# The order of eleven matmuls in the first gates of a gated unit, beside a long convolution on one core

## The chip, the core and the metric

The kernel runs on one core of one Trainium2 chip. The metric is the device time of one execution in microseconds (us). TensorE (PE) multiplies; its weight loads are listed apart (PEld). VectorE (DVE), ScalarE (ACT) and GpSimd (POOL) compute on tiles, SyncE (SP) starts transfers. The engines run side by side and wait for one another.

## The reference

The input x (2048 tokens of 448 numbers) is normalised per token. Two branches read the normalised tokens xn, and the output is the sum of x and both:

```python
xn = _layernorm(x, axis=-1)
return x + _A_ref(xn, ...) + _B_ref(xn, B_w_gate, B_w_up, B_w_down)
# A: a long convolution over the tokens, its kernel K made of 256 complex
#    exponentials per channel, done with FFTs of length 4096, plus u * D_skip
# B: the gated unit
g = jnp.einsum("bsd,df->bsf", x, w_gate)
u = jnp.einsum("bsd,df->bsf", x, w_up)
h = _sigmoid(g) * u
return jnp.einsum("bsf,fd->bsd", h, w_down)
```

The gated unit has 448 inputs, 1792 hidden units and 448 outputs.

## The kernel before, in words

**Two streams of work.** The convolution (`conv`) and the gated unit (`glu`) are two Python generators. A loop at the end of `s4d_glu_kernel` takes a step from the one that has done the smaller share of its work, so that the code's order interleaves them. That order is not the final one: the program is built with `schedule_with_timeline_sim=True`, so a planner lays out each engine's list of instructions. It takes planned durations and picks, whenever an engine is free in the plan, the ready instruction of the highest priority. Priority follows the order of the code; `hp()` moves an instruction 300 places ahead, and `tc.issue_after(i)` keeps an instruction behind another one on its engine. Once laid out, each engine's list is fixed, and the engine works it off in order.

**Stages.** First the tokens are loaded, normalised, transposed and split (0 to some 40 us). Meanwhile `prep` computes the exponents of the convolution kernel on DVE, ACT and POOL, up to about 124 us. Then `kgen` makes the kernel K chunk by chunk (TensorE at L524 and L600, DVE at L586 to L588), to about 540 us. Then `spectra` multiplies in the frequency domain and transforms back (L883, L910, L945). The gated unit fills TensorE throughout.

**The gated unit.** It takes 1024 tokens at a time (`half` 0 and 1), as two blocks t = 0 and 1 of 512 tokens, and runs over 14 slices f of 128 hidden units, in groups of three or two (`FCH`). For each (f, t) `gate` computes the two products of a slice, gate (i = 0) and up (i = 1), each in one PSUM bank `gu` (four buffers). Then ACT computes `th` (a tanh, L701), DVE `hf` (L704), ACT `hh` (L709) and DVE `hl` (L711). After a group, L801 multiplies with w_down into `po`, and DVE adds it to `acc` (L806). In half 0 the first group's order is (f 0, t 0), (f 1, t 0), (f 0, t 1), (f 1, t 1), and so on; t = 1 comes with the second block of tokens.

**Split numbers.** Each float32 operand is kept as a high part in a reduced format and a low remainder, and a product is the sum of high x high, high x low and low x high. The 448 inputs are three rows of 128 (index k) and one of 64. For the three: `xh[:, k]` and `xl[:, k]`. For the 64 that are left, `xr` holds the high part in partitions 0 to 63 and the low part in 64 to 127, so one matmul does both. Weights are `wh` and `wl`; `wh` is made by ACT from the loaded weights (L743), `wl` by DVE (L745 or L747).

**How x comes.** `x_transpose` transposes four blocks of 128 tokens with TensorE (L210). For each k, ACT copies the high part (L219) and DVE subtracts for the low part (L220); last come xr's high half by ACT (L222) and its low half by DVE (L223). For the first tokens (t = 0) and the second (t = 1) this is done at the start of the kernel.

**The order in a gate.** Each of the two accumulations is eleven matmuls in one bank, in the order of a list: wh x xh (k = 0, 1, 2), wh x xr, wl x xh (three), wl x xr, wh x xl (three).

Of the kernel before, what the change touches and what calls it, by code (L numbers as in the profile page):

```python
# [130 lines left out]
def s4d_glu_kernel(ctx, tc, io):  # L131
# [488 lines left out]
    def w_load(f, raw=None, eng=nc.sync):  # L620
        fs = slice(128 * f, 128 * f + 128)
        if raw is None:
            raw = pg.tile([128, 2, 4, 128], F32, name="wraw", bufs=1)
        for i, nm in enumerate(("B_w_gate", "B_w_up")):
            w = io[nm]
            eng.dma_start(raw[:, i, 0:3], w[0:384, fs].rearrange("(k p) f -> p k f", p=128))
            for h in range(2):
                eng.dma_start(raw[64 * h : 64 * h + 64, i, 3], w[384:448, fs])
        return raw

    def rd_load(f, rd=None, eng=nc.sync):
        if rd is None:
            rd = pg.tile([128, D], F32, name="rd", bufs=RB)
        eng.dma_start(rd, io["B_w_down"][128 * f : 128 * f + 128])
        return rd

    def w_low():
        return pg.tile([128, 2, 4, 128], F32R, name="wl", bufs=2)

    def d_low():  # L640
        return pg.tile([128, D], F32R, name="dl", bufs=FCH[0] + 1)

    def kept(t, d, f):
        for i in range(2):
            flat = t[i].rearrange("p i k f -> p (i k f)") if len(t[i].shape) == 4 else t[i]
            yield flat.bitcast(F32), d[i, f]
# [29 lines left out]
            for i in range(2):  # L676
                nc.scalar.dma_start(x1_d[:, row(b + i, g)], to[64 * i : 64 * i + 64])

    def gate(w, xs, to, between=None, behind=False):
        wh, wl = w  # L680
        xh, xl, xr = xs
        pgu = []
        for i in range(2):
            ps = psg.tile([128, 512], F32, name="gu", bufs=4)
            mm = [(wh[:, i, k], xh[:, k]) for k in range(3)]
            mm += [(wh[:, i, 3], xr)]
            mm += [(wl[:, i, k], xh[:, k]) for k in range(3)]
            mm += [(wl[:, i, 3], xr)]
            mm += [(wh[:, i, k], xl[:, k]) for k in range(3)]
            order = turns if behind and i == 1 else sp_mm if glu_on else None  # L690
            with tc.issue_after(order[0].ins) if order else nullcontext():
                for n, (a_, b_) in enumerate(mm):
                    glu_mm[:] = [nc.tensor.matmul(ps, a_, b_, start=(n == 0), stop=(n == len(mm) - 1))]  # L693
            pgu.append(ps)
            if i == 0:
                yield 2.5
                if between:
                    between()
        th = pg.tile([128, 512], F32, name="th", bufs=1)
        with hp(HP):  # L700
            marks[0] = nc.scalar.activation(th, pgu[0], AF.Tanh, scale=0.5)  # L701
        hf = pg.tile([128, 512], F32, name="hf", bufs=1)
        with hp(HP):
            marks[1] = v.scalar_tensor_tensor(hf, th, 1.0, pgu[1], ALU.add, ALU.mult)  # L704
        hfs.append(marks[1])
        hh = pg.tile([128, 512], F32R, name="hh", bufs=2 * FCH[0])
        hl = pg.tile([128, 512], F32R, name="hl", bufs=2 * FCH[0])
        with hp(HP):
            nc.scalar.copy(hh, hf)  # L709
        with hp(HP):  # L710
            v.tensor_tensor(hl, hf, hh, ALU.subtract)  # L711
        to.append((hh, hl))

    def glu():
        for half in range(2):
# [4 lines left out]
            for fs_ in ORDER[half]:  # L720
                fc, f0 = len(fs_), fs_[0]
                wts, ws, hs = [], [], [[], []]
# [12 lines left out]
                for n_, (f, t) in enumerate(order):  # L735
                    if t == 0:
                        wh = pg.tile([128, 2, 4, 128], F32R, name="wh", bufs=2)
                        if half == 0:
                            first = len(raws) == 2
                            raw, rd = raws.pop() if raws else (w_load(f), None)  # L740
                            wl = w_low()
                            with hp(HP):
                                nc.scalar.copy(wh, raw)  # L743
                                if first:
                                    v.scalar_tensor_tensor(wl, raw, lim[:, 0, 0:1], wh, ALU.mult, ALU.subtract)  # L745
                                else:
                                    v.tensor_tensor(wl, raw, wh, ALU.subtract)  # L747
                            if f not in RAW:
                                for t_, d_ in kept((wh, wl), wt_d, f):
                                    nc.sync.dma_start(d_, t_)  # L750
                        elif f in RAW:
                            raw, wl = w_load(f, eng=nc.gpsimd), w_low()
                            nc.gpsimd.tensor_copy(wh, raw)
                            nc.gpsimd.tensor_tensor(wl, raw, wh, ALU.subtract)
                        else:
                            wl = w_low()
                            for t_, d_ in kept((wh, wl), wt_d, f):
                                nc.sync.dma_start(t_, d_)
                        ws.append((wh, wl))
                    between = (lambda s_=mid[n_]: step(*s_)) if cross and mid[n_] else None  # L760

                    yield from gate(ws[f - f0], xq[2 * half + t], hs[t], between, half == 0 and (f, t) == (1, 0))
                    if t == 0:
                        dh = pg.tile([128, D], F32R, name="dh", bufs=FCH[0])
                        if half == 0:
                            rd = rd or rd_load(f)
                            dl = d_low()
                            with hp(HP), tc.issue_after((act if f == 1 else marks)[0].ins):
                                nc.scalar.copy(dh, rd)
                            nc.gpsimd.tensor_tensor(dl, rd, dh, ALU.subtract)  # L770
                            if f not in RAW:
                                for t_, d_ in kept((dh, dl), dt_d, f):
                                    nc.sync.dma_start(d_, t_)
                        elif f in RAW:
                            dl = d_low()
                            rd = rd_load(f, pg.tile([128, D], F32, name="rdw", tag="wraw", bufs=1), nc.gpsimd)
                            nc.gpsimd.tensor_copy(dh, rd)
                            nc.gpsimd.tensor_tensor(dl, rd, dh, ALU.subtract)
                        else:
                            dl = d_low()  # L780
                            for t_, d_ in kept((dh, dl), dt_d, f):
                                nc.sync.dma_start(t_, d_)
                        wts.append((dh, dl))
                    yield 2.5
                    for s_ in end[n_] if cross else ():
                        step(*s_)
                    if cross:
                        yield 2
# [304 lines left out]
    xq, psc, raws, acl, marks, slots, pqs = list(x_first), [], [], [], [None, None], {}, []  # L1093
    W1s, GGs, act = [], [], []
    gens = [conv(), glu()]
    total = [sum(Y0) + 11 * WP + 8 * WX + 34 + NCK * WK + HOLE + 17 * WS, 2 * (4 + NFT * 14.8) - HELD]
    done = [0.0, 0.0]
    done[0] += next(gens[0])
    held = False
    while any(g is not None for g in gens):  # L1100
# [4 lines left out]
        try:  # L1105
            w = next(gens[i])
# [31 lines left out]
```

## Time and profile before

| What | Value |
|---|---|
| Median of three runs | 751.43 us (747.39 to 751.76) |
| The profiled execution, its own time | 754.2 us |
| Its span, first to last instruction | 752.3 us |
| Mean granted TensorE clock | 0.983 |
| ACT busy | 421.6 us (56%) |
| HBM read, written | 69.64 MB, 43.84 MB |
| Mean transfer rate | 153 GB/s |

A row of the timeline gives the start in us, the length in us, the engine, the line of the code, the operation, the written tile and the read tiles with their shapes, a count if several were merged, and in brackets the idle time before it with what ended it. Merged rows of matmuls show the length of the group. The lengths of matmuls overlap, as they are pipelined: the distance of their starts says what one costs. A row of the waits names the waiting line, what it waited for, the total, the number of times and the longest. Waits are inferred from semaphore events; where several were awaited, the last counts.

### The profile page before, as it was taken

The page shows a single profiled execution, that of the slowest core. Times are in us where ns is not written, and L with a number is a line of the kernel's source. Part 1 is how long each engine was busy: PE and PEld are TensorE (multiplying, and loading weights), DVE is VectorE, ACT ScalarE, POOL GpSimd, SP SyncE. Part 2 cuts the span into 40 slices and gives each one's busy share as a digit, 9 for nine tenths or more (in the row PEclk, how much of TensorE's full clock was granted, in tenths as well). Part 3 has the DMA queues.
Part 4 walks back from the last instruction along what each step waited for, and adds up shares of the span by engine and source line. Part 5 has one row for each costly group of instructions (what it writes and reads, how often), then busy time and mean ns, then how long its engine had stood idle before and what let it go on. Part 6 is the DMA issues. An engine that isn't in the chain of part 4 may idle for free.

```text
span 752.3 us, 19390 instructions
## 1 busy us (share of the span) xinstructions
PE 703.2 (93%) x7892; PEld 552.4 (73%) x7892; DVE 559.1 (74%) x776; ACT 421.6 (56%) x650; POOL 343.9 (46%) x423
## 2 busy tenths in 40 slices
PE   3898998999999999999999999999899999997994
PEld 2665787887777886666878887888777787775783
DVE  5899995689789989758668888878964554663553
ACT  3546383587687878785576776777543222322310
POOL 2110074865786885747346676566445002520001
PEclk9998999999999999999999999999999999999998
DMA  9956357254144442466722223122158999999756
GB/s 206 232 143 172 96 152 225 70 170 144 49 135 138 146 120 94 144 160 186 240 95 90 81 98 117 52 90 87 30 153 245 253 248 230 247 246 237 160 152 168
DMA packets 90760, 114.75 MB, mean 153 GB/s; under 512 B 11888, under 2 KB 78640, under 8 KB 90416
## 3 DMA queue, kind: packets, MB, share of 16 engines
q1 hardware_dynamic: 79056, 89.11, 43.9%
q10 hardware_dynamic: 9040, 18.24, 8.2%
q0 software_dynamic: 2576, 6.17, 3.1%
q8 instruction: 62, 1.02, 0.6%
q14 instruction: 26, 0.21, 0.1%
HBM read 69.64 MB, written 43.84 MB: 151 GB/s over the span
## 4 chain that ended last, share of the span: by engine, by line
PE 63%; DVE 14%; DMA 9%; ACT 4%; issue 4%; SPq 3%; POOL 2%; ACTq 0%; DVEq 0%; POOLq 0%
PE gu L693 25%; PE po L801 13%; PE ko L600 7%; PE tr L524 6%; PE sp L883 5%; PE pv L910 3%; DMA v_d<-vt 2%; DVE Et L587 2%; DVE Et L586 2%; DMA vp<-v_d 2%; DVE Ft L588 2%; DVE pm L438 1%; PE kp L551 1%; DMA sx<-x_d 1%; DMA skl<-sk_d 1%
## 5 line engine op out<-in xcount | busy, mean ns | idle before, releaser
L501 POOL TENSOR_TENSOR me<-me,pm 128x32 f32<-128x32 f32 (+1 forms) x168 | 136.5, 813 | 128.1 <-DVE Et L587 116.3
L501 POOL TENSOR_TENSOR mf<-mf,pm 128x64 f32<-128x64 f32 (+1 forms) x112 | 105.5, 942 | 4.5
L693 PE MATMUL gu<-xh,wh 128*128 128x512 f32 x336 | 99.1, 402 | 2.3 <-DVE acc L806 1.1
L693 PE MATMUL gu<-xl,wh 128*128 128x512 f32 x336 | 97.0, 392 | 0.0
L693 PE MATMUL gu<-xh,wl 128*128 128x512 f32 x336 | 96.4, 393 | 0.0
L586 DVE TENSOR_TENSOR Et<-me,S 128x1024 f32<-128x1024 f32 x56 | 81.3, 1451 | 18.9 <-ACT S L536 15.5
L587 DVE TENSOR_TENSOR Et<-me,S 128x1024 f32<-128x1024 f32 x56 | 80.6, 1439 | 19.6 <-ACT me L514 18.2
L801 PE MATMUL po<-dh,hh 128*128 128x448 f32 x224 | 85.9, 383 | 2.1 <-DVE hf L704 2.1
L533 ACT ACTIVATE S<-tr 128x1024 f32<-128x1024 f32 x56 | 57.7, 1031 | 49.0 <-PE tr L524 42.6
L801 PE MATMUL po<-dl,hh 128*128 128x448 f32 x224 | 83.8, 374 | 0.0
L801 PE MATMUL po<-dh,hl 128*128 128x448 f32 x224 | 83.0, 372 | 0.0
L588 DVE TENSOR_TENSOR Ft<-mf,S 128x1024 f32<-128x1024 f32 x56 | 76.4, 1364 | 6.1 <-PE ko L600 4.4
L709 ACT CAST hh<-hf 128x512 fp32r<-128x512 f32 x56 | 35.0, 624 | 80.2 <-DVE hf L704 70.0
L600 PEld LDWEIGHTS ko<-Et,Ft 128*32 128x32 f32 x3584 | 54.2, 110 | 31.8 <-issue 17.1
L693 PEld LDWEIGHTS gu<-xh,wh 128*128 128x128 f32 x336 | 61.4, 189 | 20.9 <-issue 5.1
L600 PE MATMUL ko<-Et,Ft 128*32 128x64 f32 x3584 | 65.7, 221 | 10.7 <-DVE Ft L588 6.2
L693 PEld LDWEIGHTS gu<-xh,wl 128*128 128x128 f32 x336 | 63.4, 189 | 14.4 <-DVE pl L309 0.7
L693 PEld LDWEIGHTS gu<-xl,wh 128*128 128x128 f32 x336 | 63.0, 188 | 14.2 <-issue 0.7
L524 PE MATMUL tr<-sel,ph 128*128 128x512 f32 x224 | 66.0, 416 | 3.5 <-DMA ph<-ph_d 2.2
L536 ACT ACTIVATE S<-S,hpi 128x1024 f32<-128x1024 f32 x56 | 65.4, 1168 | 0.0
L806 DVE SCALAR_TENSOR_TENSOR acc<-po,acc 128x448 f32<-128x448 f32 x80 | 48.0, 615 | 23.4 <-PE po L801 23.2
L704 DVE SCALAR_TENSOR_TENSOR hf<-th,gu 128x512 f32<-128x512 f32 x56 | 38.2, 681 | 34.9 <-PE gu L693 33.7
(198 smaller groups left out, 1299.3 us busy)
## 6 DMA issues: line engine op xcount, KB each, us to landing
sk_d<-sk ACTq DMA_DIRECT2D x14, 512.0 KB
sx<-x_d SPq DMA_DIRECT2D x32, 224.0 KB
skl<-sk_d SPq DMA_DIRECT2D x16, 448.0 KB
vp<-v_d SPq DMA_DIRECT2D x16, 448.0 KB
v_d<-vt SPq DMA_DIRECT2D x62, 112.0 KB
wt_d<-wh SPq DMA_DIRECT2D x9, 512.0 KB
wt_d<-wl SPq DMA_DIRECT2D x9, 512.0 KB
wl<-wt_d SPq DMA_DIRECT2D x9, 512.0 KB
```

Source lines behind the costliest of these rows:

```text
L501: ins = nc.gpsimd.tensor_tensor(m[:, :, w + a : 2 * w : n], m[:, :, a:w:n], par(base + i).unsqueeze(2).to_broadcast([128, 4 * DC, w // n]) ...
L524: nc.tensor.matmul(ps[:, h], ph[:, cn % 2, 128 * h : 128 * h + 128], sel[:, i], start=(i == 0), stop=(i == 1),)
L533: nc.scalar.activation(rows(cs), pv, AF.Abs)
L536: sins[:] = [nc.scalar.activation(cs, cs, AF.Sin, scale=-TWO_PI, bias=hpi)]
L586: v.tensor_tensor(Et[:, :, :, 32:64], two(me[:, :, 32:64]), S[:, 1::-1], ALU.mult)
L587: v.tensor_tensor(Et[:, :, :, 0:32], two(me[:, :, 0:32]), S[:, 1:3, :, ::-1], ALU.mult)
L588: fts[:] = [v.tensor_tensor(Ft, two(mf), S[:, 3:5], ALU.mult)]
L600: mm = nc.tensor.matmul(ko[32 * j : 32 * j + 32, sl], Ft[:, cc, DC * h + 4 * q + j], Et[:, cc, DC * h + 4 * q + j], start=(k == 0), stop=( ...
L693: glu_mm[:] = [nc.tensor.matmul(ps, a_, b_, start=(n == 0), stop=(n == len(mm) - 1))]
L704: marks[1] = v.scalar_tensor_tensor(hf, th, 1.0, pgu[1], ALU.add, ALU.mult)
L801: glu_mm[:] = [nc.tensor.matmul(po, a_[:, bs], w_, start=(n == 0), stop=(n == 3 * fc - 1))]
L806: v.scalar_tensor_tensor(acc[:, b], po, 0.5, acc[:, b], ALU.mult, ALU.add)
```

## The change

`gate` gets an argument `first`. The call in `glu` sets it for slice f = 0 in half 0, so for two calls: (f 0, t 0) and (f 0, t 1). In these, each of the two accumulations (i = 0 and 1) takes its eleven matmuls in another order: wh x xh (three), wl x xh (three), wh x xl (three), wh x xr, wl x xr. The same eleven products are summed, in another order. The first of the list starts the accumulation and the last closes it, as before. All other gates keep their order.

```diff
-    def gate(w, xs, to, between=None, behind=False):
+    def gate(w, xs, to, between=None, behind=False, first=False):
...
             mm += [(wh[:, i, k], xl[:, k]) for k in range(3)]
+            if first:
+
+                mm = mm[:3] + mm[4:7] + mm[8:] + mm[3:8:4]
             order = turns if behind and i == 1 else sp_mm if glu_on else None
...
-                    yield from gate(ws[f - f0], xq[2 * half + t], hs[t], between, half == 0 and (f, t) == (1, 0))
+                    yield from gate(ws[f - f0], xq[2 * half + t], hs[t], between, half == 0 and (f, t) == (1, 0), half == 0 and f == 0)
```

## The prediction

> **What bounds the kernel now.** I read the page first, then the table of windows by stage, TensorE's waits in the first 41 us, the timeline there, and last the chain of work. The page's span and engine shares:
>
> ```profile
> span 752.3 us, 19390 instructions
> PE 703.2 (93%) x7892; PEld 552.4 (73%) x7892; DVE 559.1 (74%) x776; ACT 421.6 (56%) x650; POOL 343.9 (46%) x423
> ```
>
> The table of windows (window, length, then busy time of each engine, granted clock, DMA share, GB/s):
>
> ```profile
> 16.30:30.00 13.70, 12.84 (x60) 9.96 (x60) 10.53 (x29) 10.58 (x19) 2.13 (x6) 1.00 1.07 237
> 30.00:41.00 11.00, 7.96 (x33) 6.04 (x33) 10.94 (x21) 4.43 (x8) 1.15 (x1) 1.00 0.86 200
> 41.00:60.00 19.00, 18.10 (x94) 12.04 (x93) 19.00 (x40) 8.15 (x12) 1.83 (x1) 1.00 0.57 161
> 60.00:83.00 23.00, 20.17 (x98) 14.81 (x98) 23.00 (x44) 16.61 (x26) 0.20 (x1) 0.85 0.51 136
> 150.00:545.00 395.00, 383.97 (x5472) 305.09 (x5471) 326.35 (x346) 288.46 (x423) 250.22 (x298) 0.99 0.37 118
> 640.00:690.00 50.00, 45.55 (x420) 33.28 (x417) 29.78 (x54) 12.87 (x26) 16.15 (x18) 0.97 1.01 243
> 690.00:753.00 63.00, 52.54 (x458) 41.13 (x457) 27.96 (x55) 12.10 (x23) 4.38 (x8) 0.96 0.69 165
> ```
>
> TensorE is busy for 703.2 of 752.3 us, so 49 us of idleness is all that a change of order can touch. It is full in the long middle (384 of 395 us), and idle at the start and in the tail. From 30 to 83 us DVE is the engine without a gap (10.94 of 11, then 19.00 of 19 and 23.00 of 23): it works through the normalisation, the gates' epilogues and the preparation of the convolution. TensorE waits for it there. The change touches only the two gates of the unit's first group f = 0 in half 0, at 16 to 25 us and at 30 to 41 us. What TensorE waits for between 16 and 41 us (waiting line, releaser, total, times, longest):
>
> ```profile
> PE gu L693 <- DVE xr L223: 2.7, 1, 2.7
> PE gu L693 <- ACT xh L219: 0.7, 1, 0.7
> PE gu L693 <- ACT wh L743: 0.4, 1, 0.4
> ```
>
> **The change part by part.** No instruction is added or removed; 11 matmuls in each of four accumulations change places. No DMA is moved, nothing on SP's or POOL's queue is passed, and no matmul gets a new input. So the price of the matmuls themselves is nothing, and all that counts is which wait each meets. The two that read xr move from places 4 and 8 to 10 and 11. What is queued behind them on TensorE now runs ahead of the wait for xr.
>
> First tile. The timeline's rows (start, length, engine, line):
>
> ```profile
> 12.90 1.28 DVE L745 SCALAR_TENSOR_TENSOR wl<-wraw,lim,wh 128x1024 fp32r<-128x1024 f32 x1
> 16.33 1.94 PE L693 MATMUL gu<-xh,wh 128*128 128x512 f32 x6
> 17.17 0.86 PE L693 MATMUL gu<-xh,wh 128*128 128x512 f32 x3
> 18.08 0.68 DVE L220 TENSOR_TENSOR xl<-kp,xh 128x512 fp32r<-128x512 f32 x1
> 18.71 0.97 PE L693 MATMUL gu<-xh,wh 128*128 128x512 f32 x3 [0.45 <-ACT wh L743]
> 18.86 0.69 DVE L223 TENSOR_TENSOR xr<-gu,xr 64x512 fp32r<-64x512 f32 x1
> 19.60 0.50 PE L693 MATMUL gu<-xr,wh 128*128 128x512 f32 x1
> 19.94 0.86 PE L693 MATMUL gu<-xh,wl 128*128 128x512 f32 x3
> 22.83 1.90 DVE L268 TENSOR_SCALAR xn<-acc,ys,zs 128x448 f32<-128x448 f32 x2
> 24.49 0.85 PE L693 MATMUL gu<-xl,wh 128*128 128x512 f32 x3
> 25.18 0.27 PE L210 MATMUL tr<-ident,xn 128*128 128x128 f32 x1
> 26.82 0.27 PE L210 MATMUL gu<-ident,xn 128*64 128x128 f32 x1
> 28.16 0.57 ACT L701 ACTIVATE th<-gu 128x512 f32<-128x512 f32 x1
> 29.71 0.69 DVE L704 SCALAR_TENSOR_TENSOR hf<-th,gu 128x512 f32<-128x512 f32 x1 [1.78 <-PE gu L693]
> ```
>
> Six matmuls run (three for each of the gate's two banks; the third starts at 17.17), then three of the next group as soon as its wh is there at 18.71, then the first xr at 19.60, right after DVE's xr ends at 19.55. So 9 are issued before 19.60, 24 after it. Twenty start between 19.94 and 24.49, so one costs 4.55/20 = 0.2275 us. In the new order a bank needs wl (there since 14.18) and then xl (the last ends at 18.76) before xr. From 17.17 on nothing holds TensorE: by 19.60 it would have issued 2 + 2.43/0.2275 = 12.7 instead of 9, which is 3.7 x 0.2275 = 0.84 us, and the restart after the xr wait (0.34 from 19.60 to 19.94 instead of 0.2275) adds 0.11. I take 0.95 us. Is it hidden? The sixteen transposes behind (25.18 to 26.82) wait only for xn, whose last piece DVE ends at 24.73; the other three pieces are earlier. Started 0.95 earlier, twelve transposes last until about 25.4, so xn does not hold the other four. Then come 11 gate matmuls, and hf at 29.71, for which DVE had idled 1.78 us. Its other input th ends at 28.73, so hf comes at 28.76: the whole 0.95 passes to DVE, which is full from there to 83 us. This term lies on the path.
>
> Second tile:
>
> ```profile
> 30.30 2.34 PE L693 MATMUL gu<-xh,wh 128*128 128x512 f32 x9 [0.69 <-ACT xh L219]
> 33.92 0.69 DVE L220 TENSOR_TENSOR xl<-kp,xh 128x512 fp32r<-128x512 f32 x1
> 34.64 0.68 DVE L223 TENSOR_TENSOR xr<-gu,xr 64x512 fp32r<-64x512 f32 x1
> 35.38 0.50 PE L693 MATMUL gu<-xr,wh 128*128 128x512 f32 x1 [2.74 <-DVE xr L223]
> ```
>
> Nine matmuls, then 2.74 us of waiting for xr. In the new order six with wl and most of the six with xl fill it: 12 x 0.2275 = 2.7 us of work comes forward. That is cover, not gain, if DVE sets the pace behind it. TensorE's waits from 41 to 83 us, from 83 to 125 us, and two rows of DVE's groups from 30 to 83 us:
>
> ```profile
> PE po L801 <- DVE hf L704: 2.1, 1, 2.1
> PE tr L279 <- ACT x1ab L290: 1.0, 1, 1.0
> ...
> PE tr L524 <- DMA ph<-ph_d: 2.2, 1, 2.2
> PE gu L693 <- DVE acc L806: 1.1, 1, 1.1
> ...
> L747 DVE TENSOR_TENSOR wl<-wraw,wh 128x1024 fp32r<-128x1024 f32 x3 | 3.6, 1195 | 0.0
> L704 DVE SCALAR_TENSOR_TENSOR hf<-th,gu 128x512 f32<-128x512 f32 x5 | 3.4, 674 | 1.8 <-PE gu L693 1.8
> ```
>
> In its old order TensorE already waits for DVE's hf (2.1) and acc (1.1) before 84 us. A TensorE that is 2.7 us ahead waits 2.7 us longer at the same places. I price the second tile at 0 and keep -2.7 as the end of the range, for the case that its lead is kept.
>
> The part with no row is the order of everything else. Each engine's list is laid out from planned durations and priorities: the six-then-three sequence above, against the code's sequence of eleven, shows that the plan moves matmuls past one another. An earlier gate in the plan moves later instructions on all engines. I bound this by the tail's transfers (rival 3), and take 0, the value nearest to the full middle, where TensorE has work whatever the order.
>
> Sum: 752.3 - 0.95 - 0 = 751.35 of span. The profiled execution took 754.2, so 753.25 for one like it; it stands 2.77 above the median of the three runs (751.43, from 747.39 to 751.76). On the median's scale the forecast is 751.43 - 0.95 = 750.5.
>
> A word on the clock, as it may turn a lead into a loss. Windows around two waits:
>
> ```profile
> 62.00:64.00 2.00, 0.76 (x2) 0.72 (x3) 2.00 (x5) 0.78 (x2) 0.00 (x0) 0.50 1.03 298
> 126.20:129.50 3.30, 3.30 (x10) 2.93 (x9) 3.27 (x7) 1.82 (x3) 2.25 (x3) 0.50 0.99 340
> 35.40:38.00 2.60, 2.60 (x11) 2.15 (x12) 2.60 (x5) 0.98 (x2) 1.15 (x1) 1.00 0.60 136
> ```
>
> After the waits near 62 and 124 us the granted clock fell to 0.50 for a while; after the 2.74 us before 35.4 it stayed at 1.00. So closing that gap wins no clock. The Trainium skill ("TensorE: Matmul & The Clock Gate", section on HAM oscillation) says that idleness of more than about 3.4 us halves the clock. The 35.4 us row agrees; the 126 us row fell after a listed wait of only 2.2 us, less than the rule's figure, and there the row decides. By the rule alone the closed gap is worth 0.95, as by the row; the longer waits for DVE are where it speaks against the change.
>
> **The rivals.** (1) The lead is kept: the plan fills it with later gates, and TensorE's full middle begins 0.95 + 2.7 = 3.65 us further on: 747.8. For it: 93% busy. Against it: DVE at 100% from 41 to 83 us.
>
> (2) The lead is spent against the preparation: gates come earlier, and their DVE work (hf at high priority) goes ahead of preparation steps. 3.65 us are 16 matmuls, 0.73 of a gate of 22; a gate costs DVE two operations of 0.674 (hf, and hl of the same shape) and half a wl of 1.195: 0.73 x 1.95 = 1.4 us. The phases (2.2 us of wait for ph at 124 us) come 1.4 - 0.95 = 0.45 later, and the longer wait costs another half-clock stretch of 3.3 us, at half speed 1.65: +2.1, so 753.5. It decides when TensorE has nothing but po left before ph lands.
>
> (3) The tail is laid out otherwise, the slower end. There the chain runs through transfers one behind another, of which this is one:
>
> ```profile
> 646.35 8.07 DMA skl<-sk_d
> ```
>
> DMA is at 1.01 share and 243 GB/s from 640 to 690 us while TensorE idles 4.45 of 50 us, and 10.5 of the last 63. If the new plan puts one load of the spectra behind one more store, the end moves by one such transfer: 751.43 + 8.07 = 759.5. It decides as soon as less gate work than that is left to fill the wait. The mirror case, one transfer sooner, gives 743.4.
>
> (4) Nothing: the 0.95 is taken up again by the wait for ph, which follows SP's queue and not TensorE: 751.4.
>
> **How the numbers follow.** Forecast 0.38, rival (1) 0.14, (2) 0.10, (3) 0.17 late and 0.07 early, (4) 0.14. About 1%, 7.5 us, is what a measurement of this kernel can tell from no change: below 743.9, above 758.9. Faster: the early case of (3), and the third of (1) that may fall there with runs that differ by 4.4 us: 0.12. Slower: the late case of (3), with a little of (2): 0.19. The rest, 0.69, is within 1%. The range 743 to 760 reaches past both ends of (3), of which half each falls outside with the scatter of runs. The likeliest case's own range is 747.8 to 752.4, from the kept lead to the forecast plus the 1.9 by which a run may stand off.
>
> **What would show it.** First tile: the xr matmuls start as the last of their bank, no wait for xr at 19.6, the transposes end by about 26 and hf for the second gate starts near 28.8. Second tile: the 2.74 us wait is gone, and TensorE's waits for DVE between 41 and 84 us grow by about as much (2.1 and 1.1 now); if they stay, rival (1) holds. The first tr at L524 should start near 123.8 instead of 124.77; later than 125.2 speaks for (2). If the start is right and the end is off by several us, the difference must show after 545 us, in the chain's transfers: rival (3). The forecast is wrong if DVE's stretch from 30 to 83 us is not shifted as a whole, or if the order of DVE's instructions in it is another.

## The result, and the profile after

| | before | after |
|---|---|---|
| Median of the timed runs | 750.92 us (4 runs, 747.39 to 751.76) | 759.60 us (4 runs, 758.33 to 760.18) |
| Ratio, with its 95% interval | | 1.0107 [1.0071, 1.0143] |
| The profiled execution, its own time | 754.2 us | 758.33 us |
| Its span | 752.3 us | 756.5 us |
| Mean granted TensorE clock | 0.983 | 0.983 |

The kernel became slower by about 1%, where 750.5 us had been forecast; 759.6 lies just inside the range. The two profiled executions differ by 4.1 us only: that of before is a long one of its kernel, that of after the shortest of its four. The traces can therefore show about half of the 8 us directly.

The page's first lines of after. The busy times are those of before to within 1.2 us (TensorE's to within 0.6), so nearly all of the 4.2 us of span is idle time:

```profile
span 756.5 us, 19388 instructions
PE 703.8 (93%) x7892; PEld 551.3 (73%) x7892; DVE 560.2 (74%) x776; ACT 420.8 (56%) x650; POOL 344.0 (45%) x423
```

The table of windows of after (window, length, busy time of PE, PEld, DVE, ACT and POOL, granted clock, DMA share, GB/s):

```profile
30.00:41.00 11.00, 10.81 (x48) 7.06 (x47) 10.60 (x20) 5.44 (x10) 1.16 (x1) 1.00 0.88 189
41.00:60.00 19.00, 16.99 (x90) 11.09 (x88) 19.00 (x41) 7.67 (x12) 5.68 (x1) 1.00 0.55 156
60.00:83.00 23.00, 11.97 (x55) 7.57 (x55) 20.08 (x40) 15.55 (x25) 0.02 (x1) 0.76 0.42 118
```

Beside the rows of before, TensorE wins 2.85 us between 30 and 41 us (10.81 against 7.96), gives 1.1 back by 60, and loses 8.2 between 60 and 83 (11.97 against 20.17, at a clock of 0.76 in place of 0.85). DVE, which had no gap there, now has 2.9 us of them. So the stage that had been bound by DVE is bound by something else. TensorE's waits from 41 to 100 us in after:

```profile
PE tr L279 <- ACT x1ab L290: 13.0, 3, 8.0
PE gu L696 <- DVE acc L809: 0.7, 1, 0.7
```

The 4.2 us of waiting in before (2.1 for hf, 1.1 for acc, 1.0 for x1ab) have become 13.7, and the releaser is now ACT. Its timeline, before and then after (an instruction's wait stands in brackets):

```profile
63.22 0.62 ACT L709 CAST hh<-hf 128x512 fp32r<-128x512 f32 x1 [3.15 <-DMA x_d<-x1ab]
63.75 0.59 ACT L701 ACTIVATE th<-gu 128x512 f32<-128x512 f32 x1
64.24 0.90 ACT L290 COPY x1ab<-tr 128x896 f32<-128x896 f32 x1
65.02 1.06 ACT L743 CAST wh<-wraw 128x1024 fp32r<-128x1024 f32 x1
```

```profile
65.16 1.05 ACT L746 CAST wh<-wraw 128x1024 fp32r<-128x1024 f32 x1 [7.18 <-DMA wraw<-in_B_w_up_dram]
66.11 0.90 ACT L290 COPY x1ab<-tr 128x896 f32<-128x896 f32 x1
...
68.33 0.62 ACT L712 CAST hh<-hf 128x512 fp32r<-128x512 f32 x1 [1.31 <-DVE w L352]
68.85 0.59 ACT L704 ACTIVATE th<-gu 128x512 f32<-128x512 f32 x1
```

The same four instructions stand in another order. The cast of the fifth slice's weights runs at the same moment in both (65.02 and 65.16). In after it waits 7.18 us for a load, whose last two parts SP issues from 61.2 us on in both; in before it follows the x1ab copy without a wait. Before, hh, th and the fifth x1ab copy had gone ahead of it. After, they are queued behind it: x1ab 1.9 us later and hh 5.1. (Of hh's last wait, 1.31 us, ACT spends 1.24 on issuing x1ab's two transfers, from 67.04.) On TensorE the transform that needs x1ab's buffer now stands ahead of eighteen po matmuls. In the kernel before they ran first; their first, and then both rows of after:

```profile
63.24 0.74 PE L801 MATMUL po<-dh,hh 128*128 128x448 f32 x1 [2.14 <-DVE hf L704]
```

```profile
67.06 1.77 PE L279 MATMUL tr<-xn,wx 32*64 32x448 f32 x8 [8.05 <-ACT x1ab L290]
68.76 0.74 PE L804 MATMUL po<-dh,hh 128*128 128x448 f32 x1
```

On DVE the accumulations come later in turn, and the fifth of the first group (at 82.86 in before) falls behind the preparation's second set of reciprocals. Before, then after:

```profile
82.86 1.13 DVE L806 SCALAR_TENSOR_TENSOR acc<-po,acc 128x448 f32<-128x448 f32 x2
83.92 0.68 DVE L410 TENSOR_TENSOR a<-a,b 112x512 f32<-112x512 f32 x1
84.52 3.38 DVE L315 RECIPROCAL pl<-pl 112x128 f32<-112x128 f32 x4
```

```profile
87.88 3.39 DVE L315 RECIPROCAL pl<-pl 112x128 f32<-112x128 f32 x4
...
91.79 1.16 DVE L809 SCALAR_TENSOR_TENSOR acc<-po,acc 128x448 f32<-128x448 f32 x2
```

With it the next group's first hf moves from 92.49 to 101.15. What this takes from TensorE can be counted, with the table of windows for one line of the code (window, length, busy time and number of its matmuls, clock, DMA share, GB/s): L693 (gates) up to 125, 150 and 545 us, L801 (po) up to the same, L600 (ko) from 30 to 545, in before, then L696, L804 and L600 in after:

```profile
0.00:125.00 125.00, 64.07 (x264) 0.97 0.67 172
0.00:150.00 150.00, 76.63 (x317) 0.97 0.62 161
0.00:545.00 545.00, 237.49 (x977) 0.98 0.44 130
0.00:125.00 125.00, 25.30 (x107) 0.97 0.67 172
0.00:150.00 150.00, 34.63 (x144) 0.97 0.62 161
0.00:545.00 545.00, 119.08 (x528) 0.98 0.44 130
30.00:545.00 515.00, 62.23 (x3392) 0.98 0.41 125
```

```profile
0.00:125.00 125.00, 63.68 (x260) 0.95 0.64 164
0.00:150.00 150.00, 71.24 (x291) 0.95 0.60 157
0.00:545.00 545.00, 236.39 (x968) 0.98 0.44 129
0.00:125.00 125.00, 18.33 (x72) 0.95 0.64 164
0.00:150.00 150.00, 33.84 (x144) 0.95 0.60 157
0.00:545.00 545.00, 116.28 (x522) 0.98 0.44 129
30.00:545.00 515.00, 61.67 (x3334) 0.98 0.41 124
```

A gate matmul costs 0.2275 us and a po 0.2025 (the distance of their starts at full clock). By 125 us after is behind by 4 gate and 35 po matmuls, 4 x 0.2275 + 35 x 0.2025 = 8.0 us of work; by 150 us by 26 gate matmuls, 5.9 us; by 545 us by 9 gate, 6 po and 58 ko matmuls, 9 x 0.2275 + 6 x 0.2025 + 58 x 62.23/3392 = 4.3 us. The span is 4.2 us longer. So about half of the 8.0 us is won back by 545 us, and the rest stays to the end; the tail adds nothing. The two traces bear this out: in the order of their operations and tiles (buffer numbers left out) the lists of all engines, and SP's list of transfers, differ up to 151 us and are the same from there on.

### The profile page after: what moved, and what is told of

Read it like the earlier page. It is cut to its first block, busy times and chain, and to the rows that moved or that the text cites. A ratio compares the mean times of both kernels' runs of the same rounds, so it can differ in the third digit from the quotient of the medians.

```text
span 756.5 us, 19388 instructions
## 1 busy us (share of the span) xinstructions
PE 703.8 (93%) x7892; PEld 551.3 (73%) x7892; DVE 560.2 (74%) x776; ACT 420.8 (56%) x650; POOL 344.0 (45%) x423
## 4 chain that ended last, share of the span: by engine, by line
PE 61%; DMA 15%; DVE 13%; ACT 5%; issue 2%; SPq 1%; POOL 1%; ACTq 0%; DVEq 0%; POOLq 0%
PE gu L696 25%; PE po L804 13%; PE ko L600 7%; PE tr L524 7%; PE sp L886 4%; DMA vp<-v_d 3%; DMA sx<-x_d 2%; PE pv L913 2%; DMA tb<-in_c_tab_dram 2%; DMA v_d<-vt 2%; DVE Et L587 2%; DMA wraw<-in_B_w_gate_dram 1%; DVE Ft L588 1%; PE kp L551 1%; DMA xe<-in_A_u_dram 1%
## 5 line engine op out<-in xcount | busy, mean ns | idle before, releaser
L501 POOL TENSOR_TENSOR me<-me,pm 128x32 f32<-128x32 f32 (+1 forms) x168 | 134.5, 801 | 128.2 <-DVE Et L587 116.9
L696 PE MATMUL gu<-xh,wh 128*128 128x512 f32 x336 | 100.2, 403 | 0.9 <-DVE acc L809 0.7
L696 PE MATMUL gu<-xl,wh 128*128 128x512 f32 x336 | 97.8, 395 | 0.0
L696 PE MATMUL gu<-xh,wl 128*128 128x512 f32 x336 | 96.1, 394 | 0.0
L804 PE MATMUL po<-dh,hh 128*128 128x448 f32 x224 | 85.8, 383 | 0.0
L804 PE MATMUL po<-dl,hh 128*128 128x448 f32 x224 | 83.5, 373 | 0.0
L804 PE MATMUL po<-dh,hl 128*128 128x448 f32 x224 | 82.8, 372 | 0.0
L600 PEld LDWEIGHTS ko<-Et,Ft 128*32 128x32 f32 x3584 | 54.3, 110 | 31.8 <-issue 18.8
L696 PEld LDWEIGHTS gu<-xh,wh 128*128 128x128 f32 x336 | 61.5, 190 | 19.3 <-issue 5.1
L600 PE MATMUL ko<-Et,Ft 128*32 128x64 f32 x3584 | 66.0, 221 | 9.2 <-DVE Ft L588 6.0
L696 PEld LDWEIGHTS gu<-xh,wl 128*128 128x128 f32 x336 | 63.3, 189 | 14.5 <-DVE mv L247 0.7
L696 PEld LDWEIGHTS gu<-xl,wh 128*128 128x128 f32 x336 | 63.0, 189 | 14.5 <-issue 0.7
L524 PE MATMUL tr<-sel,ph 128*128 128x512 f32 x224 | 65.7, 415 | 1.0 <-ACT S L535 0.8
```

Source lines behind the costliest of these rows:

```text
L501: ins = nc.gpsimd.tensor_tensor(m[:, :, w + a : 2 * w : n], m[:, :, a:w:n], par(base + i).unsqueeze(2).to_broadcast([128, 4 * DC, w // n]) ...
L524: nc.tensor.matmul(ps[:, h], ph[:, cn % 2, 128 * h : 128 * h + 128], sel[:, i], start=(i == 0), stop=(i == 1),)
L600: mm = nc.tensor.matmul(ko[32 * j : 32 * j + 32, sl], Ft[:, cc, DC * h + 4 * q + j], Et[:, cc, DC * h + 4 * q + j], start=(k == 0), stop=( ...
L804: glu_mm[:] = [nc.tensor.matmul(po, a_[:, bs], w_, start=(n == 0), stop=(n == 3 * fc - 1))]
```

## The experiments

Theories, by the letters used below. **A**: ACT's list costs the time, as the cast of slice 4 stands ahead of x1ab, hh and th. **B**: the first tile does, as its normalisation now waits behind the first gate's hf. **C**: any plan that is laid out anew costs something, whatever its order. **D**: DVE's list does, as the fifth accumulation stands behind the reciprocals. Times are medians, beside those of before on the same chip. The ratio with its 95% interval is estimated from all their executions, and is not exactly the quotient of the two medians. A hold (`issue_after`) names one instruction, but the planner lays out anew what comes after it; by the lists in the traces, the lists of all engines can differ from there on.

**Which half of the change?** e1 gives the new order to the first tile only, e2 to the second only.

```diff
-half == 0 and f == 0)
+half == 0 and (f, t) == (0, 0))    # e1
+half == 0 and (f, t) == (0, 1))    # e2
```

> Only the first tile (f 0, t 0) takes the new order. Theory A (ScalarE's list): the loss of the whole change comes from the cast of wh for slice 4, which the plan put ahead of x1ab, hh and th on ScalarE, where it waits 7.2 us for its weights. Here it stands behind x1ab and ahead of hh and th, so TensorE should not wait 8 us at the tr of L279, but some 3 to 6 us at po for hh; total between the two kernels, 751 to 757 us. Theory B (the first tile itself: VectorE's list has hf and ex ahead of xn, hf of the second gate 0.6 us late): all of the loss is here, 758 to 760 us. Theory C (any new plan moves the end by up to 1%, through the tail): no particular value, and no wait in 55 to 70 us that explains it.

Measured: 760.51 us beside 752.12, ratio 1.0099 [1.0065, 1.0132].

> Only the second tile (f 0, t 1) takes the new order. The cast of wh for slice 4 now stands well behind x1ab, hh and th. Theory A: no long wait on ScalarE before 70 us, the 2.74 us wait of TensorE for xr is gone, total 747 to 752 us. Theory B: 750.5 to 751.5 (nothing lost, lead given back to VectorE). Theory C: anything from 743 to 760.

Measured: 755.17 us, 1.0024 [0.9996, 1.0051]. The first tile alone carries the loss, more of it than A had expected; e2 can't be told from before, though its median lies above A's range and B's. In e2 the wait of 2.74 us is gone, and its lead is not seen in the time. In e1's trace the cast stands ahead of hh and th too, though behind x1ab, and TensorE's waits at L279 are 6.8 us for x1ab and 2.3 for x1c.

**The cast put back in its place.** e3 is the changed kernel, with the cast of slice 4 kept behind the fifth x1ab copy and the sixth th. e4 does the same to the kernel before, where that order stands already.

```diff
+                            behind = [specs[4], ths[5]] if f == 4 else []
-                            with hp(HP):
+                            with hp(HP), ExitStack() as held_:
+                                for i_ in behind:
+                                    held_.enter_context(tc.issue_after(i_.ins))
```

> The changed kernel, with the cast of wh for slice 4 held behind the fifth x1ab copy and the sixth th on ScalarE. Theory A: the 7.2 us wait of ScalarE for wraw no longer blocks x1ab; TensorE's wait at tr L279 falls from 8.0 to about 1 us, total 749 to 753 us. Theory B: the loss stays, 757 to 760, as the first tile is the same. Theory C: anything from 743 to 760, not tied to the wait.

Measured: 752.75 us beside 752.12, 1.0023 [0.9988, 1.0058]. The time is in A's range. TensorE's wait for x1ab is shorter, though not the 1 us expected; the two longest waits from 30 to 125 us:

```profile
PE tr L279 <- ACT x1ab L290: 4.9, 2, 3.9
PE gu L696 <- DVE acc L813: 2.8, 1, 2.8
```

> The kernel before with the same hold on the cast of wh for slice 4. Its list around that place is the one it had anyway (x1ab, then the cast), but the plan further on is laid out anew, with many lines in another order. Theory A: 749 to 753, no difference beyond noise, as the waits before 85 us are the same. Theory C: a new plan alone moves the time by some us, either way.

Measured: 751.19 us, 0.9977 [0.9945, 1.0008]. One held instruction, with what the planner moves behind it (the lists of after and e3 differ from 65 to 151 us), takes back about four fifths of the loss. e4 shows that the hold itself costs nothing. It says nothing of C: contrary to what was expected, its lists hold the same operations on the same tiles in the same order as those of the kernel before, on every engine (buffer numbers left out). B falls, as e3 has the late normalisation and the late hf (30.4 us) that after has.

**Is that all?** e7 is e1 with e3's hold. e8 is e3 with the first step of `exp` (L298) held behind the last normalisation, which cures the delay of B.

```diff
-        v.tensor_scalar(ex, ex, ...)
+        with tc.issue_after(last_xn[0].ins):
+            v.tensor_scalar(ex, ex, ...)
```

> The first tile alone in the new order, with the cast of wh for slice 4 held behind the fifth x1ab and the sixth th. Theory A: the loss of the first tile alone (760.5) falls to 750 to 754. Theory B (hf and ex ahead of xn on VectorE in the first tile): the loss stays, 757 to 761, since these are ahead here as well.

Measured: 757.99 us beside 753.06, 1.0073 [1.0041, 1.0105].

> The changed kernel with the hold on the cast for slice 4, and the first step of exp (L298) held behind the last xn of the second block on VectorE. If the first tile's lead was lost to VectorE's list, the second block's transposes end near 26 us instead of 27.6, hf of the second gate starts near 29 instead of 30.3; total 0.5 to 1.5 us below the held kernel (752.8): 750.5 to 752.5, and it could reach the kernel before. If the first tile's place does not matter: 752 to 753.5.

Measured: 760.45 us, 1.0100 [1.0072, 1.0128]. Both are slow, e7 in B's range and e8 above both of its ranges. In e7 the fifth acc runs at 90.9 us and po waits 4.1 us for acc. In e8 the second gate's hf comes at 29.2 us and the cast is behind hh and th, and yet it is slow: A alone isn't the whole. TensorE's longest waits in e8 from 30 to 125 us:

```profile
PE gu L697 <- DVE acc L814: 7.2, 1, 7.2
PE po L809 <- DVE hf L709: 4.1, 1, 4.1
```

Here the fifth acc runs at 90.2 us, behind all eight reciprocals, and the gates that need its bank wait. This is what led to theory D.

**Each order by itself, in the kernel before.** e9 holds the fifth and sixth acc of the kernel before behind the last reciprocal, and leaves the code otherwise as it is.

```diff
-            v.reciprocal(...)
+            rec[:] = [v.reciprocal(...)]
...
-                        with hp(HP):
+                        naccs[0] += 1
+                        with hp(HP), tc.issue_after(rec[0].ins) if naccs[0] in (5, 6) else nullcontext():
```

> The kernel before, its gates unchanged, with the fifth and sixth acc of the first group (VectorE, line of acc) held behind the last reciprocal of the preparation's second half. Nothing else is moved in VectorE's list up to there. Theory D (the fifth acc is the point: it frees the PSUM banks of the next group's gates, and in every slow kernel so far it comes at 90 to 92 us, in the others at 81 to 87): the fifth acc moves from 82.9 to about 88, the seventh hf from 92.5 to about 98, total 755 to 760 us. Theory A (ScalarE's cast alone) and C (the plan at large): 749 to 754.

Measured: 754.55 us beside 750.99, 1.0048 [1.0017, 1.0078], just under D's range and above that of A and C. Its longest wait:

```profile
PE gu L693 <- DVE acc L807: 4.7, 1, 4.7
```

The 1.1 us for acc have become 4.7, and the median is 3.6 longer. e10 puts three small activations (each with a table load) behind the fourth x1ab copy on ACT and hh, th and the fifth x1ab behind them, so that the cast of slice 4 falls ahead of them, between the second activation and the third. e11 is its control: two such activations, with which the cast stays behind; apart from them its lists are those of before.

```diff
+            if x1s[0] == 4:
+                for i in range(3):      # e11: 2
+                    with tc.issue_after((stall or [cp])[0].ins):
+                        stall[:] = [nc.scalar.activation(junk, hpi, AF.Silu if i % 2 else AF.Arctan)]
...
-        with hp(HP):
+        with hp(HP), tc.issue_after(stall[0].ins) if gates[0] == 6 else nullcontext():
```

> The kernel before with three one-column activations on ScalarE behind the fourth x1ab copy, and the fifth hh, the sixth th and the fifth x1ab held behind them, so that the cast of wh for slice 4 falls ahead of these; all loads of the phases as in the kernel before. Theory A: 756 to 761. Theory D: it costs only as far as the fifth acc is late (over 88 us); if that stays below 86, 750 to 754.

Measured: 755.24 us, 1.0043 [1.0012, 1.0075].

> The same with two activations; the cast stays behind. Both theories: 749 to 753.

Measured: 752.41 us, 0.9995 [0.9966, 1.0024]. e10 lies just under A's range and above D's, with its fifth acc at 85.4 us; e11 is as expected. ACT's list and TensorE's wait in e10:

```profile
65.86 1.04 ACT L749 CAST wh<-wraw 128x1024 fp32r<-128x1024 f32 x1 [1.32 <-issue]
66.92 1.28 ACT L298 ACT_TABLE_LOAD   x1
...
68.32 0.60 ACT L715 CAST hh<-hf 128x512 fp32r<-128x512 f32 x1
```

```profile
PE po L807 <- ACT hh L715: 3.5, 1, 3.5
```

hh starts at 68.32 where e11 has it at 62.81, and a kernel that has nothing of the change is 0.43% slower. Not all of this lateness is the cast's: the third activation with its table load takes 1.5 us between the cast and hh, and the profiled execution was some 1.4 us late already at the fourth x1ab copy (60.60 beside 59.17 in before), after a stretch at half clock that is shown in the last section. So hh late on ACT, and acc late on DVE, are each enough to cost 3 to 4 us; what the cast alone would cost isn't separated. An earlier form of this pair, e5 and e6, also loaded fewer of the phases per block (three and two of six), so their times are not those of the whole computation and say little of A:

> The kernel before, its gates unchanged; ScalarE gets three one-column activations (with table loads, some 1.5 us each, results unused) behind the fourth x1ab copy, and the fifth hh, the sixth th and the fifth x1ab copy are held behind them. In the plan the cast of wh for slice 4 then falls in front of hh, th and x1ab by itself, as in the changed kernel. Theory A (a cast that waits for its weights at the head of ScalarE's list costs the time): hh starts near 67.5 us instead of 63.2, TensorE does some 4 to 6 us less gate work by 83 us, total 756 to 761 us. Theory B or C (the first tile, or the plan at large): 749 to 754.

Measured: 753.85 us beside 753.06, 1.0009 [0.9979, 1.0038].

> The same with two activations instead of three: the cast stays behind hh, th and x1ab in the list. Theory A: 749 to 753, since ScalarE was idle for 3 us at that place. If the dummies themselves cost what the run with three shows, this one is slow as well, 754 to 758.

Measured: 750.40 us, 0.9963 [0.9936, 0.9990]. e5 missed A's range; beside e6 it is slower by about as much as e10 beside e11, but the two also differ in what they load.

**Both orders together, and each mended within the change.** e13 has e9's and e10's edits in the kernel before. e12, e14 and e15 start from the changed kernel; in all three the reciprocals of the two halves are held behind the fourth and the sixth acc, and a `yield` stands ahead of them in place of behind. e12 has e8's two holds as well, e14 only that of the cast, e15 none.

```diff
-        pieces(pl)
+        yield
+        with tc.issue_after(accd[3 + 2 * h].ins):
+            pieces(pl)
...
-        yield
```

> The changed kernel with the hold on the cast for slice 4 and on ex, which took 760.5 with its fifth acc at 90.2 us, and now the reciprocals of L316 held on VectorE behind the fourth acc (first half) and the sixth (second half). Theory D: the fifth acc comes at 81 to 86 us, the seventh hf at 91 to 95, total 749 to 754 us. If it stays at 757 to 761, the fifth acc is not what costs.

Measured: 759.81 us beside 750.99, 1.0094 [1.0058, 1.0129].

> The kernel before with both late orders put in by hand: the three one-column activations that put the cast of the fifth slice's weights ahead of hh, th and the fifth x1ab copy on ScalarE (as in e10), and the fifth and sixth accumulations behind the last reciprocal on VectorE (as in e9). Theory AD (these two orders, at about 3 us each, are what the change loses): the costs add up as far as they don't overlap, 757 to 760 us beside 751 to 752 before, ratio 1.007 to 1.011. Rival (the two waits share their time, and the change loses something else besides): 754 to 756 us, ratio 1.004 to 1.006, as for each alone.

Measured: 756.44 us beside 751.71, 1.0053 [1.0020, 1.0085].

> The changed kernel with the cast of the fifth slice's weights held behind th and the x1ab copy (as in e3) and the reciprocals held behind the fourth and the sixth accumulation (as in e12), without the hold of ex that e12 had. If the hold of ex was what kept e8 and e12 slow: 750 to 754 us, ratio 0.998 to 1.004. If the reciprocals' delay itself costs (the preparation ends later): 756 to 760, ratio 1.006 to 1.010.

Measured: 750.59 us, 0.9993 [0.9956, 1.0031].

> The changed kernel with the reciprocals alone held behind the fourth and the sixth accumulation; the cast of the fifth slice's weights stays where the changed kernel has it. Theory AD: half of the loss goes, 754 to 757 us, ratio 1.004 to 1.007, with hh and th still behind the cast. Rival (the order of DVE counts for nothing in the changed kernel, since po is late anyway): 758 to 761, ratio 1.008 to 1.011.

Measured: 759.11 us, 1.0107 [1.0074, 1.0141]. e13 and e15 came out in the ranges of their rivals, e14 in the first of its two, and e12 where it was to speak against D. In e14 the whole loss is gone, though the lists of TensorE, ACT, DVE and POOL all differ from those of before: so a new plan need not cost anything, and C falls. The hold of ex is the one edit that e12 has beyond e14, so what the planner makes of that hold makes e12 slow. In e15 DVE's order alone is mended (the fifth acc runs at 87.5 us, ahead of the second set of reciprocals) and nothing is won. TensorE's longest waits from 30 to 125 us in e15, then in e14, then in e12:

```profile
PE tr L279 <- ACT x1ab L290: 13.2, 3, 8.1
```

```profile
PE tr L279 <- ACT x1ab L290: 5.0, 2, 4.0
PE po L809 <- DVE acc L814: 1.6, 1, 1.6
```

```profile
PE po L810 <- DVE hf L710: 4.2, 1, 4.2
PE gu L698 <- DVE acc L815: 4.2, 1, 4.2
PE tr L279 <- ACT x1ab L290: 2.3, 2, 1.3
```

e15 keeps after's waits for x1ab. e14 has 5 us of them, but not those for xr and ph: all its listed waits from 30 to 125 us come to 7.6 us, where before has 9.8 and after 15.2. e12 has hardly any for x1ab, but waits twice for DVE, whose list the hold of ex has shifted once more.

**What follows.** In the changed kernel the cast's place on ACT decides: moved back alone, it leaves 0.23% (e3); with DVE's order mended too nothing (e14); and without it nothing is won (e15). Between e15 and e14 the hold of the cast is the only edit, and it is worth the whole loss. From e1 to e7 the same hold wins only 0.26 points, as waits for acc stand there in place of those for x1ab. D is a second way to the same loss, shown in e9 and seen in e8, and its order on DVE is not the cause in after. The two seem not to add up (e13: 0.53% against 0.43% and 0.48%), as if their waits shared their time, but the three intervals are too wide to show it. e13 does not reach after's 1.07%: its TensorE waits 4.0 us for hh where after waits 8.05 for x1ab with a transform that stands ahead of po. That order of TensorE costs little by itself: up to 74 us e3's list is that of after, and it loses 0.23%. Whether it makes the other half where x1ab is late was not tried.

One number goes with the time in all the kernels, though loosely: the gate and po work that TensorE has started by 150 us, counted as above. The slower ones have less: after 95.4 us, e7 96.3, e1, e8 and e15 96.7, e12 97.0, e13 97.2, e9 98.1, e10 98.3. The ones that can't be told from before have more: e3 99.2, e4 101.1, before 101.3, e14 102.0, e11 102.4, e2 102.6. Within the slower ones the order isn't that of the ratios (e7 has 1.0073, e15 1.0107), and one execution can differ: e8's profiled one, the shortest of its twelve, has the span of before's, 752.3 us. (e5 and e6 are left out, since their work is another.)

No version beat both kernels: e2, e3, e4, e11 and e14 can't be told from before, and e6, which can, does less work.

## Why the prediction was wrong, point by point

**The step that failed: "The part with no row is the order of everything else ... and take 0."** It was named as a part without a row, and then bounded by a transfer in the tail. The loss lies elsewhere, in the lists of ACT, TensorE and DVE between 57 and 100 us: 9.5 us more waiting from 41 to 100 us, 8.0 us less of gate and po work by 125 us, and 4.2 us of span in the traced pair, 8 us in the median. The value nearest to the full middle was the wrong choice. The rows for a better bound were in before: the last parts of the load behind the cast were issued from 61.2 us on and the cast ran at 65.02, while hh stood ready to run at 63.22. Its swap with hh and th costs hh up to the cast's end less hh's start, 66.1 - 63.2 = 2.9 us (an estimate from these rows), and more for what TensorE has queued behind; measured, hh came 5.1 us later.

**First tile, -0.95 us: wrong in sign.** The order came out as described. The xr matmuls run last in their bank and nothing waits for xr at 19.6. But the forecast took DVE's list for fixed. It isn't:

```profile
22.91 0.69 DVE L707 SCALAR_TENSOR_TENSOR hf<-th,gu 128x512 f32<-128x512 f32 x1 [0.41 <-ACT th L704]
23.52 1.72 DVE L298 TENSOR_SCALAR ex<-ex,lim 112x514 f32<-112x514 f32 x1
25.15 0.92 DVE L268 TENSOR_SCALAR xn<-acc,ys,zs 128x448 f32<-128x448 f32 x2
```

The first gate ends sooner, so its hf and a step of `exp` go ahead of the last xn, which ends at 26.07 in place of 24.73. TensorE waits 1.29 us for it, and the second gate's hf comes at 30.34: 0.6 us late, not 0.95 early. "xn does not hold the other four" was the sentence that failed. Its price is small: e3 and e14 have this delay and lose little or nothing.

**Second tile, 0 us: right.** The wait of 2.74 us is closed: matmuls that stood behind xr run ahead of it, and xr is used at 36.01 without a wait. TensorE is 2.85 us busier between 30 and 41 us, and this lead does not reach the end: e2 (+0.24%) and e14 (-0.07%), both with intervals that hold no change, aren't shorter. The reason given, that DVE sets the pace and the lead becomes longer waits, is borne out by e2: from 30 to 125 us the 2.74 us and the 2.2 for ph are gone, but po's wait for hf is 3.6 in place of 2.1 and L279's for x1ab 3.9 in place of 1.0, and all the listed waits come to 9.1 us beside 9.8. "So closing that gap wins no clock" was read from one execution, and another shows otherwise (last section).

**The rivals.** (1) is refuted by e2 and e14, where nothing of the lead is seen in the time. (2), a loss through the start of the phases at L524, had the right sign and the wrong mechanism: L524 starts at 125.64 us, past the 125.2 that was to speak for it, but no wait for ph is listed there, and the loss has been made 40 us sooner. (3) gave the right time, 759.5, for a wrong reason: from 151 us on the lists, SP's transfers among them, are those of before, so no tail was laid out otherwise, and the 4.3 us of missing work at 545 us already account for the 4.2 us of span. A right number stood beside a refuted cause, and it is luck that the range, which was drawn out to hold that cause, holds 759.6.

**The signs to look for** were well chosen: "the forecast is wrong ... if the order of DVE's instructions in it is another" came true, with the order of ACT's instructions to be added.

**Still open:** why the medians differ by 8 us where the two profiled executions differ by 4.1, and how much of after's loss is TensorE's own order. The granted clock may be part of the first: after's four executions were granted 0.977 to 0.983, 0.980 in the mean, and 34 executions of before on one chip 0.984. At TensorE's 704 us such a difference is about 3 us (an estimate that takes its work to stretch with the clock). Whether the change brings the lower clock isn't shown; e2 was granted 0.979 and can't be told from before. That the planner moved the cast ahead because it took the weights to be there sooner is an argument from how it works, and no run shows it.

## What to carry to other kernels

Where a planner lays out every engine's list, an edit that costs nothing in its own place can still reorder lists 30 us later; compare the lists of all engines before the sum, and bound the unknown by the longest wait that a late input could put at the head of a list, with all that is queued behind it. Closing a wait ahead of a stage that another engine paced won nothing here. When the loss is found, put the suspected order by hand into the kernel before (e9, e10) and take it out of the kernel after (e3, e14, e15): the first shows what it can cost, the second whether it is the cause. Look in each trace whether the lists came out as meant: e4's did not change at all, and e10's cast did not come alone.

## What the runs showed of the hardware

**The clock.** In TensorE's wait of 8.05 us from 59 to 67 us the granted clock fell to half. The window of after:

```profile
62.00:68.00 6.00, 0.94 (x8) 0.30 (x8) 5.56 (x10) 1.85 (x2) 0.00 (x0) 0.50 0.30 89
```

The po matmuls that follow start 0.37 us apart until 71.92 and 0.20 from there on. The Trainium skill ("TensorE: Matmul & The Clock Gate", section on HAM oscillation) says that an idle stretch of more than about 3.4 us halves the clock; a halved clock in a wait of 8.05 us agrees, though it was down 3 us after the wait's start. Other rows differ, and there they decide. In before the same po matmuls ran at half speed, from 63.24 to 67.89, after a wait of 2.14 us that another of 1.03 us preceded; so the loss of clock is not new in after, where they ran at half speed from 68.76 to 71.92. And one and the same wait for xr left the clock at 1.00 in before (2.74 us, the prediction's window from 35.40 us) and was followed by half of it in e10 (2.75 us), whose lists up to there are those of before:

```profile
37.00:38.00 1.00, 1.00 (x4) 0.50 0.40 144
```

So the length of one wait does not settle the clock in these runs, and a closed gap may win clock in one execution and none in another.

**GpSimd beside VectorE.** One and the same subtraction on POOL took 1.83 us in before and 5.68 in after (spans on POOL are rough in these profiles):

```profile
52.28 1.83 POOL L770 TENSOR_TENSOR dl<-rd,dh 128x448 fp32r<-128x448 f32 x1 [14.29 <-ACT dh L769]
```

```profile
51.49 5.68 POOL L773 TENSOR_TENSOR dl<-rd,dh 128x448 fp32r<-128x448 f32 x1 [13.69 <-ACT dh L772]
```

In both it ends 1.0 us after DVE's last instruction with two inputs in SBUF ahead of the one-input reciprocals (L309 ends at 53.12, wl at 56.18). The Trainium skill ("SBUF — State Buffer", section "SBUF: two separate sides") says that such DVE instructions, and those in a two-port mode, and a GpSimd instruction lock each other out of a shared pair of ports for their whole length; these two rows agree. It need not cost time: in e14 the same instruction takes 5.57 us, and nothing is lost.
